# Output head of a cached-attention decode step: one product after a VectorE reduction, or four products after a ScalarE copy, with the loads of x on GpSimd's queue

## The chip, the cores and the metric

One core of a Trainium2 chip runs one launch of the kernel. The core has TensorE (PE, products into PSUM), VectorE (DVE), ScalarE (ACT), GpSimd (POOL) and SyncE (SP), each with its own instruction queue, and 16 DMA engines that all queues share. The metric is device time in microseconds for one execution. Three runs of the kernel before gave 661.82, 661.88 and 662.24 us, median 661.88.

## The reference

For each of two sequences (B = 2, one new token each, D = 512) the token x goes through a layer norm. The attention branch computes q = x·wq for 32 heads of 128, and attends over a cache of 32,768 keys and values for 8 key-value heads; four query heads share one of them:

```python
scores = einsum("bhqd,bhkd->bhqk", q, k) * (Dh ** -0.5)
o = einsum("bhqk,bhkd->bhqd", softmax(scores), v)
s = o.reshape(B, Sq, Hq * Dh) @ wo
g = silu(layer norm, w3, gelu, w4, residual, of the normed x)   # the w1/w2 part is zero for one position
return x + s * g
```

With a sequence length of one, the shifted parts in front of w2 are all zero, so w1 and w2 are not read. Nearly all the data is the cache: 2 × 8 pairs of one K block and one V block, 8 MB each, in bf16.

## The kernel before, in words

The work has three stages.

**Prologue.** SP queues wq, w3, w4 and the first K block. ACT's queue loads x twice: once as two rows (`x_bf`) for the layer norm, and once as four pieces into rows 0, 32, 64 and 96 of `x4_bf` (lines 264 and 265), a layout that only the very last addition (`out4`) uses; these four wait until GpSimd has cleared `x4_bf`. The prologue computes q for all heads, lays it out as masks, and runs the small MLP branch to the gate g.

**Sixteen groups.** A group is one pair (sequence, key-value head). Its K block and V block are spread over 128 partitions, 256 keys on each. K is held in three half-block slots (`kbuf`), V in two half blocks (`vbuf`). In a group:

- DVE transposes the two halves of K in 8 steps each (L481) into four buffers `T`. It waits for K (`t_k`), and from the fifth step on for a buffer that TensorE has freed (`t_used`).
- TensorE makes the scores of each half, 32 products into a bank `sc` (L550). Late in the first half it signals `s_half`, on which SP queues the next K block.
- DVE takes row maxima (`peak`, L464 and L466), TensorE spreads them (L562), DVE forms the shift, ACT takes the exponentials (L411), DVE transposes them to `pt` (L502).
- TensorE sums the exponentials with a product with ones (L566, into `S`), and then makes the value products, 64 of them, into the bank `o` (L575). The last signals `s_pv`, on which SP queues the next V block.
- DVE reduces `S` to the denominators and takes the reciprocals `rec` (L506, L510), right after its transposes of `pt`.

**The head output.** In bank `o` each row holds four 128-wide pieces, of which one counts. What is left of group m is done inside group m + 1. SP hands on `s_pv` as `t_o`. After the fourth transposition of the first half, DVE runs `head_ob`: it waits for `t_o`, multiplies `o` by a 0/1 mask `row_t` (L442) and adds the four pieces to `obm` (L446). Between the halves TensorE makes one fp32 product (`head_oT`, L526), which adds up the rows of each head. After the fourth transposition of the second half, DVE takes the row maxima of the first half and runs `head_on`, which multiplies by `rec` (L438). TensorE spreads the result (`head_xp`, L531), and DVE and GpSimd put it into `oX`.

After the last group the same steps run once more in `pe_output`, with the output products (L599) around them: `wo` comes in three parts, rows 0 to 3, 4 to 6 and 7 of eight, each with a semaphore of its own. Sixteen products belong to each row. The products of the first part stand between `head_oT` and `head_xp`. Then DVE multiplies by the gate and adds x (L517, L518), and two small transfers write the output.

**What sets the order.** Every engine's order is written out by hand. TensorE's program is in blocks with branches: `pe_turn` sends the first turn to the prologue and the others to `pe_groups`; both end in a jump to `pe_next`, which counts the turn and goes back to `pe_turn` or on to `pe_output`. `pe_output` holds a branch with a hint behind the first part of `wo`. SP's queue is in order: for each group the K transfer waits for `s_half`, the V transfer for `s_pv`, then `t_o` is raised. The last K block and the last V block are queued as two halves each.

Of the kernel before, what the change touches and what calls it, by code (L numbers as in the profile page):

```python
# [18 lines left out]
VT = 4  # L19
# [75 lines left out]
def kernel(  # L95
# [58 lines left out]
    obm = sb("obm", [128, Dh], F32)  # L154
# [19 lines left out]
    row_t = sb("row_t", [128, VT], F32)  # L174
# [55 lines left out]
    t_d, t_o = sem("t_d"), sem("t_o")  # L230
# [15 lines left out]
    with tc.tile_critical(no_gpsimd_drain=True):  # L246
# [16 lines left out]
        e_g0 = po.op(lambda e: e.memset(g4[:, :], 0.0))  # L263
        for n in range(NQ):
            ac.op(lambda e, n=n: e.dma_start(out=x4_bf[32 * n:32 * n + B, :], in_=A_x[:, 0, n * QW:(n + 1) * QW]), e_x4z, inc=(d_x4, 16))


        ve.op(lambda e: e.memset(o[:, :], 0.0), inc=(t_o, 1))
# [29 lines left out]
        ve.op(lambda v: v.tensor_reduce(out=row_t[:, :], in_=sel_o[:, :, :], axis=AX.X, op=ALU.add), (ve.sem, ve.n))  # L298
# [89 lines left out]
        for m in range(1, NG):  # L388
# [13 lines left out]
            nc.sync.sem_inc(t_o, 1)  # L402
        for i, (a, c) in enumerate(wo_parts):
            sp.op(lambda e, a=a, c=c: e.dma_start(out=wo3[:, a:c, :], in_=wos[:, a:c, :]), (s_pv, NG - 1), inc=(d_wo[i], 16))
        sp.wait((s_pv, NG))
        nc.sync.sem_inc(t_o, 1)


        for m in range(NG):
            for i in range(NPART):  # L410
                ac.op(lambda v, i=i: v.activation(  # L411
                    out=ep[i][:, :], in_=sc[i][:, :], func=ACT.Exp, scale=inv_sqrt_dh, bias=shift[:, :], accum_out=rs[:, i:i + 1]),
                    (s_shift, m + 1), e_tf if m == 0 else None, inc=(t_e, 1))

# [21 lines left out]
        def head_on():  # L436
            take(nc.vector, t_oT, 2)
            nc.vector.tensor_mul(out=on[:, :], in0=oT[:, :], in1=rec[:, :]).then_inc(t_on, 1)  # L438

        def head_ob():  # L440
            take(nc.vector, t_o)
            nc.vector.tensor_mul(  # L442
                out=ob[:, :].rearrange("p (t d) -> p t d", t=VT), in0=o[:, :].rearrange("p (t d) -> p t d", t=VT),
                in1=row_t[:, :].unsqueeze(2).broadcast_to([128, VT, Dh])).then_inc(t_d, 1)
# [25 lines left out]
        ve.op(lambda v: v.memset(rec[:, :], 1.0), inc=(t_oT, 1))  # L470
        with nc.Fori(0, NG // 2, engines=[DVE], hint_back_edge=True):
            for par in range(2):
                for i, h in enumerate(order(par)):
# [3 lines left out]
                    for r in range(NR):  # L477
# [6 lines left out]
                        if i == 0 and r == 3:  # L484
                            head_ob()
# [10 lines left out]
                for i, h in enumerate(order(par)):  # L496
# [8 lines left out]
                take(nc.vector, t_S)  # L505
                nc.vector.tensor_reduce(  # L506
                    out=den[:, :], in_=S[:, 0:NPART * rep].rearrange("p (i h) -> p h i", h=rep),
# [139 lines left out]
```

## Time and profile before

| | |
|---|---|
| median of three runs | 661.88 us |
| the profiled execution | 662.16 us, span of the trace 660.0 us |
| TensorE products busy | 423.8 us, 64% of the span |
| VectorE busy | 404.0 us, 61% |
| ScalarE busy | 29.6 us, 4% |
| GpSimd busy | 9.7 us, 1% |
| data read | 280.50 MB, 425 GB/s over the span |
| granted TensorE clock, mean | 0.828 |

The span is the time from the first to the last instruction of the trace; 2.16 us of the execution lie outside it. All times below are microseconds from the start of the span. In a row of the timeline the columns are start, duration, engine, line, operation, output and inputs, how many instructions are merged, and in brackets the idle time before the row with what ended it. "DVEq" or "PEq" there means that the engine's own queue was waiting on a semaphore.

### The profile page before, as it was taken

How to read it: one execution, taken by the hardware profiler on the slowest of the kernel's cores; microseconds unless marked ns; L12 is line 12 of the kernel's file. 1: busy time of each engine (PE TensorE's matmuls, PEld its weight loads, DVE VectorE, ACT ScalarE, POOL GpSimd, SP SyncE). 2: the span in 40 equal slices, each digit the busy share in tenths (PEclk: the TensorE clock that was granted, in tenths of full speed). 3: DMA queues.
4: the chain of work that ended last, by engine and by line, in shares of the span. 5: the costliest groups of instructions: out<-in, count | busy, mean ns of one | idle time of the engine just before them, and what ended most of it. 6: DMA issues, size and time to landing. Idle time of an engine off the chain costs nothing. (4 is left out here: it accounts for less than half of the span.)

```text
span 660.0 us, 6591 instructions
## 1 busy us (share of the span) xinstructions
PE 423.8 (64%) x2412; PEld 151.6 (23%) x2412; DVE 404.0 (61%) x571; ACT 29.6 (4%) x72; POOL 9.7 (1%) x42
## 2 busy tenths in 40 slices
PE   1637396666739666684965668496566848656965
PEld 0112132222213222221321222132122213212323
DVE  5349293773929477392946739294673919468761
ACT  1100000000000000000000000000000000000000
POOL 1000000000000000000000000000000000000000
PEclk9859788796978879697877969677796977779897
DMA  8999999999999999999999999999999999999994
GB/s 361 442 438 441 445 437 421 417 445 441 445 433 417 425 445 441 441 429 422 429 445 441 441 421 429 429 445 441 437 425 429 429 445 441 433 425 419 435 414 167
DMA packets 6458, 280.57 MB, mean 425 GB/s; under 512 B 682, under 2 KB 692, under 8 KB 1716
## 3 DMA queue, kind: packets, MB, share of 16 engines
q1 hardware_dynamic: 6408, 280.50, 98.3%
q8 instruction: 2, 0.03, 0.0%
q14 instruction: 4, 0.03, 0.0%
q10 hardware_dynamic: 44, 0.01, 0.0%
HBM read 280.50 MB, written 0.00 MB: 425 GB/s over the span
## 5 line engine op out<-in xcount | busy, mean ns | idle before, releaser
L481 DVE STREAM_TRANSPOSE T<-kbuf 128x1024 int32<-128x1024 int32 x256 | 293.9, 1210 | 151.7 <-DVEq L461 151.7
L550 PE MATMUL sc<-T,z 128*128 128x512 bf16 x1024 | 295.8, 424 | 137.1 <-PEq L461 128.2
L550 PEld LDWEIGHTS sc<-T,z 128*128 128x128 bf16 x1024 | 92.6, 103 | 325.8 <-issue 268.0
L575 PE MATMUL o<-vbuf,pt 128*16 128x512 bf16 x1024 | 92.7, 542 | 0.0
L411 ACT ACTIVATE ep<-sc,shift 128x512 bf16<-128x512 f32 x32 | 21.7, 683 | 581.0 <-DVE shift L495 581.0
L575 PEld LDWEIGHTS o<-vbuf,pt 128*16 128x16 bf16 x1024 | 30.8, 119 | 54.2 <-issue 47.2
L566 PE MATMUL S<-sm,ones_f 128*128 128x8 f32 x32 | 9.0, 354 | 51.8 <-PEq L461 51.8
L502 DVE STREAM_TRANSPOSE pt<-ep 128x512 bf16<-128x512 bf16 x32 | 22.6, 708 | 15.3 <-DVEq L461 15.3
L464 DVE TENSOR_REDUCE mx<-sc 128x1 f32<-128x512 f32 x32 | 21.5, 672 | 15.7 <-DVEq L461 15.7
L562 PE MATMUL S<-mxr,same_h 128*128 128x64 f32 x32 | 6.5, 284 | 22.0 <-PEq L461 22.0
L566 PEld LDWEIGHTS S<-sm,ones_f 128*128 128x128 f32 x32 | 7.9, 307 | 53.5 <-issue 53.5
L446 DVE TENSOR_REDUCE obm<-ob 128x128 f32<-128x512 f32 x17 | 17.7, 1040 | 2.5
L442 DVE TENSOR_TENSOR ob<-o,row_t 128x512 f32<-128x512 f32 x17 | 11.2, 656 | 7.6 <-DVEq L461 7.6
L562 PEld LDWEIGHTS S<-mxr,same_h 128*128 128x128 f32 x32 | 4.8, 188 | 29.8 <-issue 29.8
L506 DVE TENSOR_REDUCE den<-S 128x4 f32<-128x8 f32 x16 | 2.7, 167 | 13.7 <-DVEq L461 13.7
L466 DVE TENSOR_SCALAR mxr<-row_of,mx 128x32 f32<-128x32 f32 x32 | 7.7, 241 | 4.8
L431 POOL COPY oX<-oXs 128x4 bf16<-128x4 bf16 x15 | 2.9, 191 | 517.6 <-DVE oXs L458 517.6
L493 DVE TENSOR_REDUCE top<-S 128x1 f32<-128x64 f32 x16 | 3.6, 224 | 11.2 <-DVEq L461 11.2
L526 PEld LDWEIGHTS oT<-sel_h,obm 128*128 128x128 f32 x34 | 6.3, 188 | 5.4 <-issue 2.7
L329 PE MATMUL sc<-kbuf,xT 128*2 128x512 bf16 x32 | 3.6, 627 | 5.5 <-DMA kbuf<-in_A_wq_dram 5.5
L366 PE MATMUL sc<-vbuf,h_bf 128*2 128x512 bf16 x14 | 4.9, 522 | 2.4 <-DVE h_bf L363 2.4
L420 POOL TENSOR_TENSOR z<-qr,quad 128x64 bf16<-128x64 bf16 x16 | 4.7, 294 | 107.6 <-DVE shift L495 90.4
(80 smaller groups left out, 73.8 us busy)
## 6 DMA issues: line engine op xcount, KB each, us to landing
kbuf<-in_A_k_cache_dram SPq DMA_DIRECT2D x2, 4096.0 KB, 22.0
vbuf<-in_A_v_cache_dram SPq DMA_DIRECT2D x2, 4096.0 KB, 18.6
kbuf<-in_A_wq_dram SPq DMA_DIRECT2D x1, 4096.0 KB, 13.5
vbuf<-in_B_w_dram SPq DMA_DIRECT2D x2, 1792.0 KB, 19.2
kbuf<-in_A_wo_dram SPq DMA_DIRECT2D x1, 2048.0 KB, 27.6
kbuf<-in_A_wo_dram SPq DMA_DIRECT2D x1, 1536.0 KB, 31.0
kbuf<-in_A_wo_dram SPq DMA_DIRECT2D x1, 512.0 KB, 31.7
kbuf<-in_A_k_cache_dram SPq DMA_DIRECT2D x15, 27.0
```

The source lines that it names most:

```text
L411: ac.op(lambda v, i=i: v.activation(out=ep[i][:, :], in_=sc[i][:, :], func=ACT.Exp, scale=inv_sqrt_dh, bias=shift[:, :], accum_out=rs[:, i ...
L442: nc.vector.tensor_mul(out=ob[:, :].rearrange("p (t d) -> p t d", t=VT), in0=o[:, :].rearrange("p (t d) -> p t d", t=VT), in1=row_t[:, :]. ...
L446: nc.vector.tensor_reduce(out=obm[:, :], in_=ob[:, :].rearrange("p (t d) -> p d t", t=VT), axis=AX.X, op=ALU.add).then_inc(t_ob, 1)
L464: nc.vector.tensor_reduce(out=mx[:, i:i + 1], in_=sc[i][:, :], axis=AX.X, op=ALU.max).then_inc(t_d, 1)
L466: ins = nc.vector.tensor_scalar_mul(out=mxr[:, i, :], in0=row_of[:, :], scalar1=mx[:, i:i + 1])
L481: nc.vector.transpose(out=Ts[n % T_BUFS][:, :].rearrange("p (b t k) -> p t b k", b=NB, t=RT), in_=kt[:, r * W:(r + 1) * W].rearrange("p (t ...
L502: nc.vector.transpose(out=pt[h][:, :, :].rearrange("p r (t h) -> p t r h", h=rep), in_=ep[i][:, :].rearrange("p (t r h) -> p t r h", r=NR, ...
L526: nc.tensor.matmul(oT[:, :], lhsT=obm[:, :], rhs=sel_h[:, :], start=True, stop=True).then_inc(t_oT, 1)
L550: ins = nc.tensor.matmul(sc[i][:, :], lhsT=z[:, nb, w, zc:zc + 128], rhs=Tb[:, nb, :, w], start=(r == 0 and nb == 0 and w == 0), stop=(r = ...
L562: nc.tensor.matmul(S[:, NPART * rep:], lhsT=same_h[:, :], rhs=mxr[:, :, :].rearrange("p i r -> p (i r)"), start=True, stop=True).then_inc( ...
L566: nc.tensor.matmul(S[:, 0:NPART * rep], lhsT=ones_f[:, :], rhs=sm[:, :, :].rearrange("p i h -> p (i h)"), start=True, stop=True).then_inc( ...
L575: ins = nc.tensor.matmul(o[32 * j:32 * j + VT * rep, :], lhsT=pt[h][:, r, a * VT * rep:(a + 1) * VT * rep], rhs=vt[:, u * VT:(u + 1) * VT, ...
```

## The change

Four things are altered.

- GpSimd instead of ACT issues the four small loads of x into `x4_bf`, behind its clearing operations. One more clearing, of `ob`, goes ahead of them.
- `head_ob` with its mask `row_t` is gone. ACT copies the bank `o` to `ob` after each group, waiting for `s_pv` itself, so SP's relay `t_o` is gone too. TensorE's `head_oT` makes four fp32 products that accumulate, one for each 128-wide piece, with the selecting matrix `sel_o` in the place of `sel_h`.
- The sum of the exponentials is made after the value products instead of before them. The reduction to denominators and the reciprocal move from the end of the group into `head_on`, in the next group; `S` starts as ones.
- TensorE's program loses the block `pe_next` and the hinted branch: a group ends in the count and the branch itself, `pe_output` is one piece, and the prologue stands last in memory.

```diff
@@ prologue @@
+        po.op(lambda e: e.memset(ob[:, :], 0.0), inc=(t_ob, 1))
         for n in range(NQ):
-            ac.op(lambda e, n=n: e.dma_start(out=x4_bf[32 * n:32 * n + B, :], in_=A_x[:, 0, n * QW:(n + 1) * QW]), e_x4z, inc=(d_x4, 16))
-        ve.op(lambda e: e.memset(o[:, :], 0.0), inc=(t_o, 1))
+            po.op(lambda e, n=n: e.dma_start(out=x4_bf[32 * n:32 * n + B, :], in_=A_x[:, 0, n * QW:(n + 1) * QW]), e_x4z, inc=(d_x4, 16))
+        ve.op(lambda e: e.memset(o[:, :], 0.0))
+        ve.op(lambda e: e.memset(S[:, 0:NPART * rep], 1.0), inc=(t_S, 1))
...
-        ve.op(lambda v: v.tensor_reduce(out=row_t[:, :], in_=sel_o[:, :, :], axis=AX.X, op=ALU.add), (ve.sem, ve.n))
@@ SP @@
             load_v(m, (s_pv, m))
-            nc.sync.sem_inc(t_o, 1)
...
-        sp.wait((s_pv, NG))
-        nc.sync.sem_inc(t_o, 1)
@@ ACT, each group @@
+            ac.op(lambda v: v.copy(out=ob[:, :], in_=o[:, :]), (s_pv, m + 1), inc=(t_ob, 1))
@@ DVE @@
         def head_on():
+            take(nc.vector, t_S)
+            nc.vector.tensor_reduce(
+                out=den[:, :], in_=S[:, 0:NPART * rep].rearrange("p (i h) -> p h i", h=rep),
+                axis=AX.X, op=ALU.add).then_inc(t_d, 1)
+            take(nc.vector, t_d)
+            nc.vector.reciprocal(out=rec[:, :], in_=den[:, :]).then_inc(t_oT, 1)
             take(nc.vector, t_oT, 2)
             nc.vector.tensor_mul(out=on[:, :], in0=oT[:, :], in1=rec[:, :]).then_inc(t_on, 1)
-        def head_ob():
-            take(nc.vector, t_o)
-            nc.vector.tensor_mul(
-                out=ob[:, :].rearrange("p (t d) -> p t d", t=VT), in0=o[:, :].rearrange("p (t d) -> p t d", t=VT),
-                in1=row_t[:, :].unsqueeze(2).broadcast_to([128, VT, Dh])).then_inc(t_d, 1)
-            take(nc.vector, t_d)
-            nc.vector.tensor_reduce(
-                out=obm[:, :], in_=ob[:, :].rearrange("p (t d) -> p d t", t=VT), axis=AX.X, op=ALU.add).then_inc(t_ob, 1)
...
@@ TensorE @@
         def head_oT():
             take(nc.tensor, t_ob)
-            nc.tensor.matmul(oT[:, :], lhsT=obm[:, :], rhs=sel_h[:, :], start=True, stop=True).then_inc(t_oT, 1)
+            for t in range(VT):
+                ins = nc.tensor.matmul(
+                    oT[:, :], lhsT=ob[:, t * Dh:(t + 1) * Dh], rhs=sel_o[:, t, :],
+                    start=(t == 0), stop=(t == VT - 1))
+            ins.then_inc(t_oT, 1)
...
             take(nc.tensor, t_pt, NPART)
-            nc.tensor.matmul(
-                S[:, 0:NPART * rep], lhsT=ones_f[:, :], rhs=sm[:, :, :].rearrange("p i h -> p (i h)"),
-                start=True, stop=True).then_inc(t_S, 1)
...
             ins.then_inc(s_pv, 1)
-            nc.br("pe_next", engines=[PE])
+            nc.tensor.matmul(
+                S[:, 0:NPART * rep], lhsT=ones_f[:, :], rhs=sm[:, :, :].rearrange("p i h -> p (i h)"),
+                start=True, stop=True).then_inc(t_S, 1)
+            nc.regs_alu(turn, turn, 1, op=ALU.add)
+            nc.br_lt(turn, NG + 1, on_true="pe_turn", on_false="pe_output", engines=[PE])
...
-            in_next_block = nc.tensor.mark_branch_hint_location()
             head_oT()
             for i, (a, c) in enumerate(wo_parts):
                 if i == 1:
-                    nc.tensor.br_ne(turn, 0, "pe_output_2", "pe_turn").branch_hint(in_next_block)
-                    nc.switch_bb("pe_output_2")
                     head_xp()
```

More of the change, by code (lines that the diff above doesn't have):

```diff
@@ L153 @@
     den = sb("den", [128, rep], F32)
-    obm = sb("obm", [128, Dh], F32)
     mx = sb("mx", [128, NPART], F32)
@@ L504 @@
                         in_=ep[i][:, :].rearrange("p (t r h) -> p t r h", r=NR, h=rep)).then_inc(t_pt, 1)
-                take(nc.vector, t_S)
-                nc.vector.tensor_reduce(
-                    out=den[:, :], in_=S[:, 0:NPART * rep].rearrange("p (i h) -> p h i", h=rep),
-                    axis=AX.X, op=ALU.add).then_inc(t_d, 1)
-                take(nc.vector, t_d)
-                nc.vector.reciprocal(out=rec[:, :], in_=den[:, :]).then_inc(t_oT, 1)
-        head_ob()
         head_on()
```

10 lines of the change are left out of this document (2 added, 8 removed).

## The prediction, made before the result was known

> **What bounds the kernel now.** I read the stream of data first: the page's DMA queues and issues, the table of stretches, and the waits of SP's queue.
>
> ```profile
> q1 hardware_dynamic: 6408, 280.50, 98.3%
> kbuf<-in_A_k_cache_dram SPq DMA_DIRECT2D x15, 27.0
> vbuf<-in_A_v_cache_dram SPq DMA_DIRECT2D x15, 24.3
> 100.00:200.00 100.00, 61.57 (x361) 22.03 (x362) 56.70 (x80) 4.34 (x12) 1.46 (x6) 0.83 1.00 433
> SPq L380 <- PE o L575: 303.2, 14, 22.4
> ```
>
> SP's queue keeps the 16 DMA engines busy for 98.3% of the span. In the middle they move 433 GB/s, so a block of 8.39 MB takes 19.4 us. A K block lands 27.0 us after its issue and a V block 24.3: they are queued 7.6 and 4.9 us before the engines reach them. SP waits for TensorE (`s_pv`, 303.2 us in 14 waits) and still issues in time. In the middle of the run, then, no engine's work can shorten the time, and none lengthens it unless it delays an issue by more than 4.9 us. What is left is the start and the end. The end is read from the landings of the last blocks, the timeline from group 14 (the last but one) on, and the chain of waits.
>
> ```profile
> L397 SPq DMA_DIRECT2D kbuf<-in_A_k_cache_dram x2: 328/374/420, 594.8 to 595.2; - x2
> ...
> DMA to landing us min/median/max: 17.4/22.0/26.7
> L385 SPq DMA_DIRECT2D vbuf<-in_A_v_cache_dram x2: 327/380/433, 617.6 to 618.0; - x2
> ...
> DMA to landing us min/median/max: 13.9/18.6/23.2
> L404 SPq DMA_DIRECT2D kbuf<-in_A_wo_dram x3: 388/507/4286, 618.5 to 619.5; - x3
> ...
> DMA to landing us min/median/max: 27.6/31.0/31.7
> ...
> 650.89 1.66 PE pro L599 x64
> 652.55 0.20 PE xp L531 x4
> 652.75 1.59 PE pro L599 x54
> 654.34 1.14 issue
> 655.47 0.35 PE pro L599 x10
> ```
>
> The rows of L397 (last K), L385 (last V) and L404 (`wo`) give the first and last issue, and from issue to landing least, median and most. First issue plus least and last issue plus most: the halves of K land at 612.2 and 621.9, those of V at 631.5 and 641.2, the first and third part of `wo` at 646.1 and 651.2, and the second, a median of 31.0 behind an issue near 618.9, at 649.9. The other rows are the chain that ended last, in order of time (start, duration, what). The last data is there at 651.2, but the output products end at 655.82: at the end the kernel is 4.6 us behind its data, held by a chain of engines. That chain is what the change can touch.
>
> **The change part by part.** First the chain through the last two groups.
>
> ```profile
> 587.85 0.65 DVE L442 TENSOR_TENSOR ob<-o,row_t 128x512 f32<-128x512 f32 x1
> 589.60 9.12 DVE L481 STREAM_TRANSPOSE T<-kbuf 128x1024 int32<-128x1024 int32 x8
> 611.09 6.47 PE L575 MATMUL o<-vbuf,pt 128*16 128x512 bf16 x64
> 612.26 4.62 DVE L481 STREAM_TRANSPOSE T<-kbuf 128x1024 int32<-128x1024 int32 x4 [0.46 <-DVEq L461]
> 617.49 3.79 PE L550 MATMUL sc<-T,z 128*128 128x512 bf16 x16
> 618.61 0.69 DVE L442 TENSOR_TENSOR ob<-o,row_t 128x512 f32<-128x512 f32 x1 [1.72 <-DVEq L461]
> 620.42 9.12 DVE L481 STREAM_TRANSPOSE T<-kbuf 128x1024 int32<-128x1024 int32 x8
> 641.38 0.50 PEld L566 LDWEIGHTS S<-sm,ones_f 128*128 128x128 f32 x2 [3.35 <-issue]
> 641.90 6.42 PE L575 MATMUL o<-vbuf,pt 128*16 128x512 bf16 x64
> 642.12 0.17 DVE L506 TENSOR_REDUCE den<-S 128x4 f32<-128x8 f32 x1 [0.86 <-DVEq L461]
> 642.43 0.18 DVE L510 RECIPROCAL rec<-den 128x4 f32<-128x4 f32 x1
> ```
>
> *`head_ob` leaves DVE.* In group 14 it stands from 587.85 to 589.60: 1.75 us. *Denominators move into `head_on`*: reduction to reciprocal takes 0.31 (642.12 to 642.43), and I take the same from the reciprocal to the product, +0.62 between two rounds of transposes (bounds: the bare 0.17 + 0.18 = 0.35, and 1.2 with each of two semaphore trips as long as the 0.46 before 612.26). At the old place nobody was behind them but the next K. *The sum product moves behind the value products*, which start 0.52 earlier (641.38 to 641.90). So group 14's value products start at 611.09 − 1.75 + 0.62 − 0.52 = 609.44 and end at 615.9; the sum product takes 0.52, and the scores of group 15 start at 616.45 instead of 617.49.
>
> In group 15 `head_ob` costs more than its 1.75: DVE has made four transposes by 616.88 and then waits 1.72 us for the value products, so the fifth comes at 620.42. Without it the fifth waits for the first free buffer only, that is for 4 of the 16 products at 617.49 (3.79 × 4/16 = 0.95): 616.45 + 0.95 + 0.2 for the signal = 617.6. That is 2.8 us earlier. The next delay would be the second half of K at 621.9; DVE needs it at 617.6 + 4 × 1.14 = 622.2, just behind. With +0.62 in `head_on` and −0.52 for the sum product, the last value products start 2.7 us earlier, at 639.2. Their second half needs V at 639.2 + 3.2 = 642.4, after its landing at 641.2. They end at 648.32 − 2.7 = 645.6.
>
> *Four products instead of one* in mid-group: the page's row of L526 (below) counts two weight loads of 188 ns for each of the 17 products, so three more are 1.1 us on TensorE between the halves. DVE paces there, its four buffers (4.6 us) ahead, and `head_on` asks for the result only after four more transposes; I cost it at nothing, and at 1.1 us if that cover fails. *ACT's copy* adds a wait for `s_pv` on ACT; behind it stand the next group's exponentials, which come some 22 us later (616 to 638), so only the last copy counts. *`head_on`'s wait for the sum* holds up DVE's last four transposes, but the sum is made before the next group's first scores. *SP's relay* goes without cost, and SP's later issues were not held by it.
>
> Then the tail.
>
> ```profile
> 638.88 0.69 ACT L411 ACTIVATE ep<-sc,shift 128x512 bf16<-128x512 f32 x1 [29.37 <-DVE shift L495]
> L526 PEld LDWEIGHTS oT<-sel_h,obm 128*128 128x128 f32 x34 | 6.3, 188 | 5.4 <-issue 2.7
> 650.50 0.30 PEld L526 LDWEIGHTS oT<-sel_h,obm 128*128 128x128 f32 x2 [2.68 <-issue]
> 650.53 0.36 PE L526 MATMUL oT<-sel_h,obm 128*128 128x4 f32 x2 [2.21 <-PEq L461]
> ```
>
> Before, the relay, mask and sum take 2.18 us, from the last value product (641.90 + 6.42 = 648.32) to 650.50. After, an ACT pass over the same 128x512 bank: 0.69 by L411's row, 0.1 to 0.2 to start it, 0.1 to hand on: 0.95, to 646.55 (bounds: 0.69 alone, and 2.18 if it is as slow as the old path). The sum product, 0.52, runs beside it on TensorE. Four products at 0.32 each (one, from its first weight load to its end at 650.89, is 0.39, and the load of the next overlaps) end at 647.85 (bounds: 0.28 and 0.45 each, −0.2 and +0.5). Part one of `wo` has landed; 64 products, 1.66: 649.5. `head_xp` 0.20: 649.7. Part two lands at 649.9: a new wait of 0.2. Its 48 products at 1.59/54 = 0.029 us: 651.35. Part three has landed at 651.2; 16 products: 651.85.
>
> *The pause of 1.14 us* at 654.34 is no wait for data: 54 products had run since 652.75, 48 of part two and six of part three, and no semaphore stands between the sixteen of part three. The count of DMA queues has a row for instructions; here it stands for the whole span, for the window 0 to 5 and for the window 653 to 655.
>
> ```profile
> q8 instruction: 2, 0.03, 0.0%
> ...
> q8 instruction: 1, 0.02, 1.3%
> ...
> q8 instruction: 1, 0.02, 3.0%
> ```
>
> One such transfer comes at the start, when TensorE enters the prologue, one in the pause, none in the sixteen groups between. I read it as code of the output fetched when it was reached. After the change the output stands ahead of the prologue, so that the code behind the groups is needed, and fetched, at the start. I cost the pause at zero; the bounds are zero and 2.5 us (653, where the window begins, to 655.47, if nothing ran beside the fetch). [...]
>
> Sum against 655.82: value products −2.7, copy for relay, mask and sum −1.2, three more products +0.9, wait for part two +0.2, pause −1.1, together −3.9; by the times themselves 651.85 − 655.82 = −3.97, **−4.0 us**. Behind it L517, L518 and the write stay as they are. The profiled execution, 662.16, becomes 658.2; it lies 0.28 above the median, so against 661.88 I forecast **658.0 us**. It can't come much lower: part three at 651.2 and 16 products end at 651.65.
>
> **The start.**
>
> ```profile
> 1.53 1.19 ACTq L265 DMA_DIRECT2D x_bf<-in_A_x_dram  x4
> 20.21 0.29 POOL L420 TENSOR_TENSOR z<-qr,quad 128x64 bf16<-128x64 bf16 x1 [17.23 <-DVE qr L343]
> 32.22 0.21 DVE L374 CAST x<-x_bf 128x128 f32<-128x128 bf16 x1
> 42.41 4.62 DVE L481 STREAM_TRANSPOSE T<-kbuf 128x1024 int32<-128x1024 int32 x4 [9.33 <-DVEq L461]
> 32.38 2.50 ACTq L373 DMA_DIRECT2D g<-g  x4
> q10 hardware_dynamic: 4, 0.00, 0.0%
> ```
>
> ACT's four issues took 1.19 us and delayed only a table load. On GpSimd they come after its clearing operations, from about 3 us on; behind them in its queue is `z`, at 20.21, which TensorE reads only after 42.41. No row shows what an issue on GpSimd costs: from 0.3 us each, as on ACT, to some 10 us each before `z` would be late. The cast of x at 32.22 did not wait, and DVE's next work that counts comes at 42.41, when K lands: 10 us of cover. I take nothing. The clearing of `S`, the mask `row_t` and the first `rec` on DVE lie in the same stretch.
>
> **Rivals.** *The output's code is fetched late on the new path too.* For it: the pause exists. Against it: the transfer at the start and none in the groups. Price 1.14 to 2.5: 659.1 to 660.5. *The chain gains less and TensorE's and ACT's added steps eat it*: `head_on` at 1.2, copy at 2.18, products at 0.45 and the pause kept: 658.0 + 0.6 + 1.2 + 0.5 + 1.1 = 661.4, which is no difference (a measurement of this kernel tells about 0.2%, 1.3 us, from none). It needs all bounds at once. *Slower: x lands late.* Small loads queue behind the stream: of the four loads of g issued from 32.38 to 34.88, packets still moved after 50 (the last row, window 50 to 60), some 18 us. Four loads issued by about 8 would so be in at 26. Every microsecond after 42.4 starts the groups later; 7.6 are covered by the second K block's place in the queue and 4.0 by the gain, so beyond 54 the kernel is slower; at 57 it is 665. [...]
>
> **How the numbers follow.** Forecast 0.65 (657.2 to 659.2); code fetch 0.14; no difference 0.07; x late 0.09; slower stream 0.05. Faster 0.79, same 0.07, slower 0.14. The two slower cases, 0.14, and the tails are left out; the rest reaches from 657.2, below the bound by the last landing by half a microsecond, to 661.4.
>
> **What would show it.** No DVE row between the fourth and fifth transposes; the fifth of group 15 near 617.6; last value products near 639.2; L599 without a pause, its last products right behind the landing at 651.2. Wrong if the landings themselves move, if x's cast at 32.22 comes later than 42, or if a packet of the instruction queue stands in the tail.

## The result and the profile after

The changed kernel takes 659.29 us, median of six executions (658.06 to 660.09), against 661.85 for six of the kernel before beside it: a ratio of 0.9958, 95% interval 0.9946 to 0.9971. It is faster, by 0.42%, and the forecast of 658.0 is 1.3 us too low: the median lies 0.09 us above the 657.2 to 659.2 of the forecast's main case, and inside the 657.2 to 661.4 that the forecast spans. A second set of six, taken later, gave 658.18 (658.04 to 659.85) and a ratio of 0.9947 (0.9926 to 0.9968). The executions spread over two microseconds; what lies behind this spread is the subject of most of the experiments. The profiled execution is the slowest of the first six: 660.09, with a span of 658.3 where the prediction's sum gave 656.0 (660.0 − 4.0).

The end first: the timeline of the changed kernel, last group and output (start, duration, engine, line, what; in brackets the idle time before it and what ended it).

```profile
614.23 9.13 DVE L474 STREAM_TRANSPOSE T<-kbuf 128x1024 int32<-128x1024 int32 x8 [2.97 <-DVEq L455]
...
624.05 4.62 DVE L474 STREAM_TRANSPOSE T<-kbuf 128x1024 int32<-128x1024 int32 x4 [0.70 <-DVEq L455]
...
629.55 0.16 DVE L435 TENSOR_REDUCE den<-S 128x4 f32<-128x8 f32 x1
...
630.33 4.62 DVE L474 STREAM_TRANSPOSE T<-kbuf 128x1024 int32<-128x1024 int32 x4
...
641.34 5.37 PE L560 MATMUL o<-vbuf,pt 128*16 128x512 bf16 x64 [3.39 <-PEq L455]
...
646.76 0.59 ACT L410 COPY ob<-o 128x512 f32<-128x512 f32 x1 [6.65 <-PE o L560]
...
647.49 1.03 PE L511 MATMUL oT<-sel_o,ob 128*128 128x4 f32 x8 [0.46 <-PEq L455]
...
648.45 1.06 PE L585 MATMUL pro<-kbuf,oX 128*2 128x128 bf16 x64
...
649.44 0.25 PE L519 MATMUL xp<-on,sel_r 128*128 128x4 bf16 x4
...
652.05 1.87 PE L585 MATMUL pro<-kbuf,oX 128*2 128x128 bf16 x64 [2.36 <-DMA kbuf<-in_A_wo_dram]
```

DVE makes its first eight transposes of the last K block in one stretch, where before four were followed by 1.72 us of waiting and by `head_ob`. Behind them it waits 0.70 us for the second half of K, which by the trace landed at 623.8. The copy stands right behind the value products, four fp32 products behind the copy (the row counts two passes for each), and the second half of the output products runs without a pause. The last row's bracket is the new thing: TensorE has idled for 2.36 us, and what ended that is data. Before, the last products ran 4.6 us behind the last landing. The row of the `wo` loads (the changed kernel's line L402) gives first and last issue, and from issue to landing least, median and most.

```profile
L402 SPq DMA_DIRECT2D kbuf<-in_A_wo_dram x3: 433/507/7352, 617.4 to 618.4; - x3
...
DMA to landing us min/median/max: 30.8/34.1/34.7
```

The last part of `wo` lands at 618.4 + 34.7 = 653.1 and the products end at 652.05 + 1.87 = 653.92, 0.8 behind it. What TensorE waited for is the second part (chain of waits):

```profile
617.83 34.09 DMA kbuf<-in_A_wo_dram
651.92 0.14 issue
```

From its landing at 651.92 to the end of the 64 products are 2.0 us; the forecast had 649.9 and 651.85. The chain at the end is as short as forecast. But before, that landing was at 651.2: the data itself is 1.9 us later. The data is late from the first K block on, which shows in the first transposes, as DVE idles until the block lands (timeline at the start):

```profile
44.29 13.70 DVE L474 STREAM_TRANSPOSE T<-kbuf 128x1024 int32<-128x1024 int32 x12 [12.87 <-DVEq L455]
```

Before it was 42.41. The 1.9 us arise ahead of 44 and are never made up: q1, the queue of the loads, fills 98.7% of the 16 engines' span, and the lateness is still 1.9 at the end. What is new ahead of 44 is in the table of DMA queues: the rows of the instruction queue q8 and of the software queue for the whole span, and that of q8 in the window 28 to 33 (packets, MB, share of the time of 16 engines in the window).

```profile
q8 instruction: 7, 0.11, 0.1%
...
q0 software_dynamic: 128, 0.00, 0.0%
...
q8 instruction: 2, 0.03, 4.4%
```

Before, this queue had two transfers in the whole run (near 4 and 653), here it has seven, at 2.1, 9.0, 30.9, 31.2, 74.5, 653.0 and 658.0 by the trace, 16,384 B each. That they are TensorE's code is a reading: the trace does not say whose code a transfer carries, but the runs below change them by changing TensorE's blocks alone. Two come together 2.3 us after TensorE has ended its prologue (28.6) and goes back to the loop, and 4.4% of 16 engines for 5 us are 3.5 us for the two, 1.4 and 2.1. In the runs below, a transfer near 31 that met no other took 0.93 to 0.96; the one near 2, amid the first loads, took 1.5 to 1.9 without meeting another (1.9% to 2.4% in the window 0 to 5, six profiles). The 128 packets of the software queue are the loads of x by GpSimd, whose row has its four issues and the times from issue to landing:

```profile
L264 POOL DMA_DIRECT2D x_bf<-in_A_x_dram x4: 521/524/704, 3.4 to 5.1; - x4
...
DMA to landing us min/median/max: 7.6/9.2/10.4
```

So there are two suspects for the late landings: the code transfers near 31 (theory A), and GpSimd's queue (theory B).

The landings narrow the place down. The trace has 16 landing signals for each load, which I read as one for each DMA engine; a block counts as landed with the last of them. For the load of weights that ends at 23 us, the latest two signals are 1.31 and 1.45 us behind the median one; in the first run below, with x on ScalarE, it is 1.02 and 1.35. At the first K block they are 2.70 and 3.25 behind here, 1.19 and 1.31 there, while the median signal comes at 40.9 and 40.8. By that reading two engines of sixteen lose their time, and they lose it between 23 and 41 us.

### The profile page after: what moved, and what is told of

Read it like the earlier page. It is cut to its first block, busy times and chain, and to the rows that moved or that the text cites. A ratio compares the mean times of both kernels' runs of the same rounds, so it can differ in the third digit from the quotient of the medians.

```text
span 658.3 us, 6698 instructions
## 1 busy us (share of the span) xinstructions
PE 411.1 (62%) x2498; PEld 167.2 (25%) x2514; DVE 376.8 (57%) x538; ACT 38.9 (6%) x88; POOL 12.4 (2%) x47
## 3 DMA queue, kind: packets, MB, share of 16 engines
q1 hardware_dynamic: 6408, 280.50, 98.7%
## 5 line engine op out<-in xcount | busy, mean ns | idle before, releaser
L538 PE MATMUL sc<-T,z 128*128 128x512 bf16 x1008 | 280.7, 428 | 141.5 <-PEq L455 137.2
L538 PEld LDWEIGHTS sc<-T,z 128*128 128x128 bf16 x1024 | 101.0, 105 | 301.6 <-issue 220.6
L560 PE MATMUL o<-vbuf,pt 128*16 128x512 bf16 x1024 | 90.5, 531 | 54.2 <-PEq L455 54.2
L560 PEld LDWEIGHTS o<-vbuf,pt 128*16 128x16 bf16 x1024 | 32.9, 117 | 106.0 <-issue 98.6
L511 PEld LDWEIGHTS oT<-sel_o,ob 128*128 128x128 f32 x136 | 17.7, 191 | 3.2 <-issue 0.5
L511 PE MATMUL oT<-sel_o,ob 128*128 128x4 f32 x136 | 16.2, 243 | 0.5 <-PEq L455 0.5
L410 ACT COPY ob<-o 128x512 f32<-128x512 f32 x16 | 9.4, 586 | 111.1 <-PE o L560 111.1
L519 PE MATMUL xp<-on,sel_r 128*128 128x4 bf16 x68 | 4.1, 164 | 4.4 <-PEq L455 4.3
L567 PEld LDWEIGHTS S<-sm,ones_f 128*128 128x128 f32 x32 | 4.8, 188 | 6.9 <-issue 6.9
L407 ACT ACTIVATION_READ_ACCUMULATOR ep<-sc,shift 128x1 f32 x32 | 6.3, 196 | 0.0
## 6 DMA issues: line engine op xcount, KB each, us to landing
kbuf<-in_A_wo_dram SPq DMA_DIRECT2D x1, 512.0 KB, 34.7
```

Of the source, the lines that this page charges most:

```text
L407: ac.op(lambda v, i=i: v.activation(out=ep[i][:, :], in_=sc[i][:, :], func=ACT.Exp, scale=inv_sqrt_dh, bias=shift[:, :], accum_out=rs[:, i ...
L410: ac.op(lambda v: v.copy(out=ob[:, :], in_=o[:, :]), (s_pv, m + 1), inc=(t_ob, 1))
L511: ins = nc.tensor.matmul(oT[:, :], lhsT=ob[:, t * Dh:(t + 1) * Dh], rhs=sel_o[:, t, :], start=(t == 0), stop=(t == VT - 1))
L538: ins = nc.tensor.matmul(sc[i][:, :], lhsT=z[:, nb, w, zc:zc + 128], rhs=Tb[:, nb, :, w], start=(r == 0 and nb == 0 and w == 0), stop=(r = ...
L560: ins = nc.tensor.matmul(o[32 * j:32 * j + VT * rep, :], lhsT=pt[h][:, r, a * VT * rep:(a + 1) * VT * rep], rhs=vt[:, u * VT:(u + 1) * VT, ...
L567: nc.tensor.matmul(S[:, 0:NPART * rep], lhsT=ones_f[:, :], rhs=sm[:, :, :].rearrange("p i h -> p (i h)"), start=True, stop=True).then_inc( ...
```

## The experiments

"Together" below means that the two code transfers near 31 us overlap in the profile.

**Who issues x.** First the changed kernel with ScalarE instead of GpSimd as the issuer, and then the kernel before with GpSimd as the issuer.

```diff
-            po.op(lambda e, n=n: e.dma_start(out=x4_bf[...], in_=A_x[...]), e_x4z, inc=(d_x4, 16))
+            ac.op(lambda e, n=n: e.dma_start(out=x4_bf[...], in_=A_x[...]), e_x4z, inc=(d_x4, 16))
```

> The changed kernel with the four loads of x back on ACT's queue, nothing else. In the trace of the changed kernel the last two of the 16 engines land the first K block 2.7 and 3.3 us behind the median engine (0.9 and 1.5 before), and the lateness stays, so the last part of wo lands at 653.1 instead of 651.2. Theory A (code): two code transfers near 31 us, when TensorE goes back from the prologue, held up two engines. Then nothing moves here: lateness of the first K block about 3 us, two code transfers near 31, time 659.3 +- 0.8. Theory B (queue): GpSimd's loads made two engines late. Then the lateness falls to 1.5, the last part of wo lands near 651.2, and the time is 658.0.

658.44 us (658.01 to 659.51), ratio 0.9954 (0.9939 to 0.9969), beside 661.61 before. In the profiled execution (658.17, span 656.4) one code transfer stands in the window 28 to 33, and nothing is late: the transposes start at 42.23. The window's row, and from the chain of waits the last landing and the products behind it:

```profile
q8 instruction: 1, 0.02, 1.2%
```

```profile
617.25 33.99 DMA kbuf<-in_A_wo_dram
651.25 0.14 issue
651.38 0.62 PE pro L585 x15
```

Without lateness the last value products start at 639.48, where the prediction had 639.2, and the output products end at 652.0; the prediction had 651.85. Two of the other five executions took over 659, as some of the changed kernel do.

> The kernel before with GpSimd issuing the four loads of x, nothing else. Theory A (code): no code transfer near 31, lateness of the first K block 1.5 us, time 661.9 +- 0.4. Theory B (queue): lateness about 3, last landing near 653, time 662.5 to 663.5.

The kernel before with the opposite edit: 661.53 (659.06 to 663.8), ratio 0.9997 (0.9985 to 1.0009). No difference, no code transfer near 31, transposes from 42.39. In its profile the pause ahead of the last ten products is there as before, 1.36 us. The loads of GpSimd alone delay nothing that can be measured.

**The order of TensorE's blocks.** The kernel before, without the block `pe_next` and without the hinted branch, and nothing else changed. In the source text the prologue stands behind the output in both kernels; that it stands last in memory only without `pe_next` is the premise of this section, and no trace shows it. "New order" below means without `pe_next`, "old order" with it.

```diff
             ins.then_inc(s_pv, 1)
-            nc.br("pe_next", engines=[PE])
+            nc.regs_alu(turn, turn, 1, op=ALU.add)
+            nc.br_lt(turn, NG + 1, on_true="pe_turn", on_false="pe_output", engines=[PE])
...
-                    nc.tensor.br_ne(turn, 0, "pe_output_2", "pe_turn").branch_hint(in_next_block)
-                    nc.switch_bb("pe_output_2")
...
-            nc.br("pe_next", engines=[PE])
-        with nc.body("pe_next", valid_engines=[PE]):
...
-            nc.br_lt(turn, NG + 1, on_true="pe_turn", on_false="pe_output", engines=[PE])
+            nc.br("pe_turn", engines=[PE])
```

> The kernel before with TensorE's blocks in the order of the changed one (prologue last, no block for the count, no hinted branch), the head unchanged. Theory A (code): code transfers near 31 us and about 3 us of lateness; the pause of 1.1 us among the last output products is gone; the chain before it is that of before, so the products end near 654.7 and the time is 660.8 (659.9 to 661.9). Theory B (queue): no lateness beyond 1.5, and the same gain from the pause, 660.7. Rival to my reading of the pause: it is not code, stays, and the time is 661.9 or more.

661.36 (658.77 to 664.92), ratio 1.0002 (0.9984 to 1.0021). The chain at the end has no pause any more:

```profile
650.96 0.20 PE xp L531 x4
651.15 1.37 PE pro L597 x61
652.52 0.03 issue
```

The new order takes the pause away. That the pause was code fits all five profiles that have one, here and below: in each the products go on 1.26 to 1.39 us behind the end of the code transfer in the tail (before: 653.14 + 0.96 = 654.10, products from 655.47).

Yet the median shows no gain (the interval leaves room for 1 us), and the twelve executions lie further apart (6.2 us) than those of before beside them (659.86 to 662.63). The profiled one is among the quickest: its output products end at 652.52, 3.3 us ahead of before, and the pause is only 1.1 of that. The value products of the last two groups take 5.21 and 5.79 us; before they took 6.47 and 6.42, and in the last run of all, which has the same TensorE program and only x issued by GpSimd, 6.41 and 6.39. The granted clock differs with them. The rows are those of group 14 in this run and in that last one, each with its line in the table of stretches (there the third number from the end is the granted clock):

```profile
611.04 5.21 PE L575 MATMUL o<-vbuf,pt 128*16 128x512 bf16 x64
611.04:616.25 5.21, 5.21 (x66) 1.85 (x66) 4.38 (x6) 0.00 (x0) 0.00 (x0) 0.69 1.02 440
...
611.60 6.41 PE L575 MATMUL o<-vbuf,pt 128*16 128x512 bf16 x64
611.60:618.01 6.41, 6.41 (x66) 2.16 (x66) 4.97 (x6) 0.00 (x0) 0.00 (x0) 0.56 0.99 429
```

Duration times clock is 3.6 in both. With the head of before the end hangs on these products, so the time depends on the clock that an execution is granted there. With the new head they end ahead of the data: in its nine profiles the value products of the last group take 5.3 to 6.1 us, and TensorE still waits 0.8 to 2.5 us for the second part of `wo`. That this is why executions of the old head spread over several microseconds is likely, not shown, since those that weren't profiled have no rows.

Here too code transfers come near 31: two between 28 and 33, this time apart (28.4 and 30.7), 2.3% in the window's row instead of 4.4%, 0.93 us each, and the transposes start in time, at 42.42.

```profile
q8 instruction: 2, 0.03, 2.3%
```

**A head that is smaller, with the old order.** The changed kernel with `ob`, `sel_o`, `sm`, `ones_f`, `mxr` and `same_h` in bf16, and with `pe_next` back (without the hinted branch); x is issued by ScalarE. Each product of the head is then a single weight load: the groups by line have 68 loads of 96 ns for the 68 products, where the changed kernel has 136 of 191 ns.

```diff
-    ob = sb("ob", [128, VT * Dh], F32)
+    ob = sb("ob", [128, VT * Dh], BF16)
...
-            nc.regs_alu(turn, turn, 1, op=ALU.add)
-            nc.br_lt(turn, NG + 1, on_true="pe_turn", on_false="pe_output", engines=[PE])
+            nc.br("pe_next", engines=[PE])
```

> [...] Theory A (code): no transfer near 31, lateness 1.5 at the first K block and about 0.9 at the end, last part of wo at 651.2, output products at its heels; 657.7 to 658.3, or up to 1.1 more if the code of the last output products is again fetched when reached. It should be 1 us or more below the changed kernel with x on ACT. Theory B (queue): both the same, 658.0.

658.28 (658.20 to 658.77), ratio 0.9949 (0.9936 to 0.9963). Six executions within 0.6 us; no code transfer near 31, transposes from 42.22. The pause is back, but what is left of it is 0.51 us (chain of waits). Reckoned back from the products at 651.90, with the 1.26 to 1.39 behind a transfer and some 0.96 for the transfer, I estimate that the transfer began near 649.6, ahead of the last landing at 650.98.

```profile
617.08 33.90 DMA kbuf<-in_A_wo_dram
650.98 0.14 issue
651.12 0.27 PE pro L585 x5
651.39 0.51 issue
651.90 0.51 PE pro L585 x11
```

The same with x issued by GpSimd:

> The kernel with the head in bf16 in the block order of before, the four loads of x on GpSimd instead of ACT; that kernel on ACT had 658.28 (658.20 to 658.77), narrow enough to see half a microsecond. Theory A2: loads of x cost nothing, no code transfer near 31: 658.3 +- 0.3. Theory C: 658.8 to 659.2.

658.41 (658.13 to 658.53, seven executions), ratio 0.9951 (0.9932 to 0.997), no code transfer near 31, transposes from 42.46. GpSimd's issue costs nothing that can be measured with the new head either.

**The changed kernel again**, beside these:

> The changed kernel once more, beside the others on one chip. The first trace had two code transfers near 31 us, 0.26 apart, that took 1.4 and 2.1 us, and the last part of wo at 653.1; with x on ACT one of 0.9 us, and wo at 651.2. Theory A2 (code, by chance): how late an engine becomes depends on whether the code transfers meet on one engine that is behind already, so it differs from execution to execution; times between 658.0 and 660.1, and lateness of the first K block and time of the last landing go together. Theory C (GpSimd's loads cost 0.8 us in every execution): 659.3 again, and the kernel with x on ACT is at 658.4.

658.18 (658.04 to 659.85). The profiled execution is the one of 659.85. The window 28 to 33 and the first transposes:

```profile
q8 instruction: 2, 0.03, 4.6%
```

```profile
44.14 13.63 DVE L474 STREAM_TRANSPOSE T<-kbuf 128x1024 int32<-128x1024 int32 x12 [11.14 <-DVEq L455]
```

Together again, and late again; the five executions that weren't profiled took 658.04 to 658.70, beside the forecast of 658.0.

**The place of the sum product.** The changed kernel with the sum product ahead of the value products, and the denominators at their old place:

```diff
+            nc.tensor.matmul(
+                S[:, 0:NPART * rep], lhsT=ones_f[:, :], rhs=sm[:, :, :].rearrange("p i h -> p (i h)"),
+                start=True, stop=True).then_inc(t_S, 1)
...(value products)
-            nc.tensor.matmul(
-                S[:, 0:NPART * rep], lhsT=ones_f[:, :], rhs=sm[:, :, :].rearrange("p i h -> p (i h)"),
-                start=True, stop=True).then_inc(t_S, 1)
```

> The changed kernel with the sum product again ahead of the value products and the denominators right behind it, at the end of the group. By the prediction's terms the last value products start 0.52 later for the last group and 0.52 for the one before, and head_on is 0.62 shorter twice; so the start of the last value products moves by -0.2 to +0.5. The output waits for wo part two in the changed kernel, so the time should move by no more than +0.3: 658.3 to 659.6. If the value products were still what the end hangs on, +0.5.

658.75 (657.99 to 660.11), ratio 0.9961 (0.9946 to 0.9975): nothing that can be told from the changed kernel. The profiled execution (659.99) has the transfers together (4.4%) and its transposes from 44.22. Then the reverse, the kernel before with only the sum product moved behind the value products and the denominators in `head_on`:

> The kernel before with only the sum product moved behind the value products and the denominators into head_on; mask and sum stay on DVE, block order as before. By the prediction's terms the value products of group 14 and 15 start 0.52 earlier each and head_on grows by 0.62; the wait of DVE for the value products of group 14 goes with them: last value products 0.0 to 0.4 earlier, the sum product beside DVE's mask and sum costs nothing, pause as before: 661.2 to 661.8. So this part alone brings almost nothing, and the gain of the change must lie with mask and sum leaving DVE.

664.32 (663.36 to 667.09), ratio 1.0044 (1.0027 to 1.0061): slower, where I expected no difference. The rows of the last group (timeline):

```profile
613.79 4.62 DVE L487 STREAM_TRANSPOSE T<-kbuf 128x1024 int32<-128x1024 int32 x4 [1.18 <-DVEq L468]
...
642.59 0.70 DVE L508 STREAM_TRANSPOSE pt<-ep 128x512 bf16<-128x512 bf16 x1
...
643.59 1.88 PE L572 MATMUL o<-vbuf,pt 128*16 128x512 bf16 x16 [3.39 <-PEq L468]
```

The value products start 0.30 us after the last transposition of the weights (643.59 − 643.29). For the kernel before the same two rows give 640.56 + 0.70 and 641.90: 0.64. The move gains 0.34, not 0.52, as the wait for the signal stays, and `head_on` takes back 0.63. From the first transposition of the last K block to the last value products it is 29.80 here and 29.64 before. The rest of the loss is not in that chain: the last K block lands 1.5 us later (613.79 against 612.26, DVE idle ahead of both), though no code transfer stands near 31 and the transposes start at 42.34, and the pause is 1.64 instead of 1.14. By the landings of the K blocks the loss builds up on the way: 0.16 us at 197, 1.51 at 507. Why the stream loses it I can't say.

**What brings the transfers together?** The small-head version, x on ScalarE, with nothing but the order of the blocks as in the changed kernel:

```diff
-            nc.br("pe_next", engines=[PE])
+            nc.regs_alu(turn, turn, 1, op=ALU.add)
+            nc.br_lt(turn, NG + 1, on_true="pe_turn", on_false="pe_output", engines=[PE])
...
-            nc.br("pe_next", engines=[PE])
-        with nc.body("pe_next", valid_engines=[PE]):
...
-            nc.br_lt(turn, NG + 1, on_true="pe_turn", on_false="pe_output", engines=[PE])
+            nc.br("pe_turn", engines=[PE])
```

> [...] Theory A (two code transfers near 31 us, when TensorE goes back from the prologue to the loop, and at times both at once, which leaves the last transfer engines 1.8 us late for the rest of the run): code transfers near 31 us in the profile; the times spread from 658.0 to 660.1 as those of the changed kernel do, where the version with the old order lay within 658.2 to 658.8; no pause ahead of the last output products. If the profiled execution has the two transfers together, its first K block's lag is near 3 us and its last landing near 653.2; if it has one or two apart, 1.3 and 651.2. Rival (the order of the blocks has no effect on the start): no transfer near 31 us or no effect of it, 658.0 to 658.6 in every execution.

658.50 (657.83 to 658.86), ratio 0.9952 (0.9939 to 0.9966). The transfers near 31 are there, at 28.4 and 30.7, so the order brings them, here the loss of `pe_next` alone. They came apart, the window's row has the 2.3% of two undisturbed transfers, and the execution of 657.83 is one of the shortest of all. None of the five reached 659, so the spread that I expected did not show.

The old order with the few instructions that count the groups pushed further back, behind one branch more and a block that is never entered:

```diff
-            nc.br("pe_next", engines=[PE])
+            nc.br("pe_gate", engines=[PE])
...
+        with nc.body("pe_gate", valid_engines=[PE]):
+            nc.br_lt(turn, 99, on_true="pe_next", on_false="pe_pad", engines=[PE])
+        with nc.body("pe_pad", valid_engines=[PE]):
```

> [...]

658.15 (657.71 to 658.95), ratio 0.9947 (0.9932 to 0.9962). The queue's row for the whole span:

```profile
q8 instruction: 2, 0.03, 0.0%
```

Two transfers in all, at 4.0 and 31.0, and none in the fifteen later turns. Of the two outcomes that I had set down, transfers in many turns with 660 to 690 us, and one transfer more near the first turn with 658.0 to 658.8, the second came. The second transfer came alone at 31.0, took 0.96, and delayed little (transposes from 42.66; 42.22 and 42.46 in the two runs of the old order with the small head). There is no pause in the tail either, and no transfer in it (window 640 to 660).

All three profiles with the transfers together had GpSimd as the issuer of x, all others with the new order ScalarE. The last two runs test that: the version with the small head and the new order, and the kernel before with the new order, each with GpSimd as the issuer.

> The small-head version with the changed kernel's order of TensorE's blocks, and the four loads of x issued by GpSimd instead of ScalarE: of the version of the run before it, only the issuer of x differs. In the profiles so far the two code transfers after TensorE's prologue came together at 30.8 to 31.2 us in all three that had GpSimd issue x (the changed kernel twice, and with the sum first), with landings 1.8 us late; where ScalarE issued x they were apart (28.4 and 30.7) or only one was seen, without lateness. Theory A (the time at which the request meets the data decides, and that is a matter of one execution): together or apart, times from 658.0 to 660.1, or 657.8 to 658.9 as with ScalarE. Theory B (GpSimd's issue of x, with this order of blocks, brings the two together): together, first K block's lag near 3 us, last landing near 653, the profiled time 659.5 to 660.1, and a median above 658.7.

658.39 us (ratio 0.9957, 0.9944 to 0.997): 658.14, 658.20, 658.37, 658.41, and 659.97, 660.24. The profiled one, 658.14, has a single transfer near 31, and its transposes start at 42.55.

```profile
q8 instruction: 1, 0.02, 1.2%
```

> The kernel before with its prologue last in TensorE's memory (as in the run with the block order alone), and the four loads of x issued by GpSimd. Theory A: as the block order alone, 661.4, within 0.6, transfers together or apart. Theory B: the two code transfers together near 31 us, landings 1.8 us late, a median of 662.5 to 663.5.

661.58 (660.02 to 664.59), ratio 1.0005 (0.9992 to 1.0018), again one transfer near 31, transposes from 42.41, no pause; as the order alone. Theory B as put falls: GpSimd as the issuer does not suffice to bring the transfers together. That it makes them meet more often is not excluded: with the new head and the new order 11 of 28 executions took over 659.0 with GpSimd as the issuer, 2 of 11 with ScalarE. What the profiles of all kernels show side by side (share: the instruction queue's in the window 28 to 33):

| kernel | order | x by | transfers near 31, share | transposes from | profiled, us |
|---|---|---|---|---|---|
| before | old | ScalarE | none | 42.41 | 662.16 |
| before, x moved | old | GpSimd | none | 42.39 | 661.59 |
| before, sum last | old | ScalarE | none | 42.34 | 664.06 |
| before, order | new | ScalarE | 2 apart, 2.3% | 42.42 | 659.09 |
| before, order and x | new | GpSimd | 1, 1.2% | 42.41 | 661.23 |
| changed | new | GpSimd | 2 together, 4.4% | 44.29 | 660.09 |
| changed, again | new | GpSimd | 2 together, 4.6% | 44.14 | 659.85 |
| changed, sum first | new | GpSimd | 2 together, 4.4% | 44.22 | 659.99 |
| changed, x moved | new | ScalarE | 1, 1.2% | 42.23 | 658.17 |
| small head | old | ScalarE | none | 42.22 | 658.25 |
| small head, x | old | GpSimd | none | 42.46 | 658.27 |
| small head, count moved | old | ScalarE | 1, 1.2% | 42.66 | 658.20 |
| small head, order | new | ScalarE | 2 apart, 2.3% | 42.51 | 657.83 |
| small head, order and x | new | GpSimd | 1, 1.2% | 42.55 | 658.14 |

The late start goes with the overlap: all three profiles with it have one, none of the eleven others has; neither the order nor the issuer alone brings it. In the three, the latest two landing signals of the first K block are 2.7 to 3.3 us behind the median one, in the eleven at most 1.8. With the new head, the profiled executions with the overlap took 659.85 to 660.09, those without 657.83 to 658.27. The times of the executions that weren't profiled fit, though nothing shows what their transfers did: of those with the new head and the new order (changed kernel twice, x moved, sum first, small head with the order, and with x), 10 of 33 took over 659.0 (with the profiled ones 13 of 39); of those with the new head and the old order, none of 14 (17).

## Why the prediction was right, and where it was off

The sign held, and so did the mechanism at the end of the kernel. That the first median came out at 659.29 and not near 658.2, as the second, is partly luck: four of the first six executions took over 659, one of the second six. It is also near the price of the rival "the output's code is fetched late" (659.1 to 660.5), but no pause of that kind came. The sum itself gives 661.88 − 3.97 = 657.9; 658.0 is a rounding up. Step by step, measured in the profile of the changed kernel:

- *`head_ob` leaves DVE, and its wait in the last group goes.* From the first transposition of the last K block to the last value products: 612.26 to 641.90 before, 29.64 us; 614.23 to 641.34 after, 27.11. The gain is 2.5, the term was 2.7; in the run with x on ScalarE, whose data is in time, the last value products start at 639.48 instead of 641.90, 2.4. The fifth transposition starts some 4.6 us after the first instead of 8.2; but part of this only makes DVE idle longer ahead of the block, as it is out of work when the data comes, and the second half of K, which the prediction had just in time, is now waited for (0.70). The 0.2 for a signal in that step was my estimate, and no row shows it.
- *Denominators in `head_on`*: 629.55 to 630.33 holds three operations, 0.78, where the one at 630.41 took 0.15 before the next transposes: +0.63, forecast +0.62.
- *The sum product behind the value products*: 0.34 by the run that moved it alone, forecast 0.52. Together with the denominators it brings nothing, and the run that undid both in the changed kernel differed by nothing. So, by elimination, the gain lies with mask and sum leaving DVE for the copy and the four products; no run makes that move alone.
- *The copy on ACT*: 0.59 instead of 0.69, and 0.14 from its end (647.35) to the first product behind it (647.49), where I had taken 0.1.
- *Four products*: 1.03 against 1.28. The 64 products of the first part of `wo`: 1.06 against 1.66. This second difference is the clock and not the change: the granted clock was 1.00 here (648 to 651) and 0.50 before (651 to 653). The sum took every time of TensorE as it stood in one profile, at the clock granted there. Both gains go into the wait for the second part, 2.36 instead of 0.2, and are worth nothing, as the data is the bound: the end comes 2.0 us behind the second part of `wo` in this profile (forecast 1.95), and in the one with x on ScalarE 0.76 behind the third (652.01 − 651.25; the prediction's floor had 0.45).
- *The pause goes with the order.* It does, in every version with the new order. But the transfer in the tail does not: the changed kernel has one at 653.0, and every version with the new order one between 649.9 and 653.7, with no pause beside it. That the code behind the groups is fetched at the start, on which the zero rested, was my estimate: no trace says what a transfer carries. What the runs show is a pause of 0.15 to 1.64 us in the profiles that have one, and none with the new order.
- *The start: "I take nothing", and code "fetched at the start" at zero.* Here is the step that failed. For the loads of x it was right: each issue kept GpSimd for 0.56 us (four in 2.25), the data was in by 15.5 (5.1 + 10.4), and the two runs that moved the issue alone to GpSimd found 0.9997 and, with the small head, the same median within 0.2 us. For the code it was wrong. I had not counted on transfers at 31 us, amid the stream, 2.3 us behind the prologue's last product; the trace shows the transfers, not their reason. In some executions (13 of 39, if the times over 659.0 are taken for them) the two transfers meet, the landings are 1.8 us late from there on, and since data is the bound at the end now, 1.8 us late at 44 are nearly 2 us late at 654.

The rival "the output's code is fetched late" was wrong on place: what the transfers cost is at the start, 1.9 us at the first K block. "x late" and "slower stream" fell with the two runs on the issuer; neither shows a stream that GpSimd's loads slow (0.9997 on the kernel before; 658.41 against 658.28 with the small head). I had named moved landings as what would make the prediction wrong, and that is what the first median's 1.3 us are. I had also named a packet of the instruction queue in the tail; it came, but nothing waited for it.

The change in order and the change of the head can now be priced apart. The new head with the old order gains 3.3 us (658.28 against 661.61), all that the changed kernel gains in its second set (3.35); the bf16 of that version shortens products that end ahead of the last landing in either form (the four of the head took 0.24 us with bf16 in the profile of the version with the order as well, and 1.03 in the changed kernel's). The order shows no gain: on the kernel before, two runs with it have 1.0002 (0.9984 to 1.0021) and 1.0005 (0.9992 to 1.0018), which leaves room for 1.1 and 0.5 us, no more; with the new head the pause is half hidden behind the last landing anyway, and the order seems only to add executions that end near 660. The small head with the old order and with the moved count keep below 659.0 without exception, though their medians can't be told from that of the changed kernel's second set.

What stays open: whether two code transfers meet seems a matter of when they fall among the data, but what decides it was not found; that they delay the landings is shown by the company they keep in 14 profiles, not by a run that forces them together. Three profiles show one transfer near 31 where the same TensorE program shows two in others; why is not known. Which DMA engine carries them is not in the trace. And the stream of the version with only the sum moved is 1.5 us late for a reason that I don't know.

## What to carry to other kernels

When the data is the bound at the end, a chain is worth shortening only down to the last landing; after that, look at what delays the first landing: here 1.9 us at the first K block were 1.9 us at the last part of `wo`, 610 us later. Changing the blocks of an engine's program changed its code transfers too, from two to seven here: count the transfers of the instruction queue before and after, and see at what times they fall, as a pause taken out of the tail (1.14 us here) may be paid for at the start (1.9). When a kernel's executions lie further apart than those of the kernel beside it, one profile may be one of two cases; take a second before explaining it. And the same 64 products took 5.21 us at a granted clock of 0.69 and 6.41 at 0.56: compare durations of two profiles only with the clock beside them.

## What the runs showed of the hardware that I had not expected

- Near 31 us a code transfer of 16,384 B among saturated data took 0.93 to 0.96 us alone; two that met took 1.4 to 2.1 us each, about 3.5 together. With them the latest two of the 16 landing signals of the first K block came 1.5 to 1.9 us further behind the median one than in the run with x on ScalarE, and the last part of `wo` landed 1.9 us later (653.1 against 651.2).
- With the old order the instruction queue had two transfers in the whole run, in all six profiles: with the moved count none came behind 31.0, through 15 turns and 620 us. With the new order, where the loop has no `pe_next`, it had six or seven in the six profiles whose whole span was read, one or two of them near 31 in all eight. Why is not shown.
- The same 64 value products of a group took 4.90 us (from 611.55) to 6.54 us (from 495.61) in the changed kernel's profile, as the granted clock was 0.73 and 0.55 while they ran.
- Four loads issued by GpSimd, 0.56 us each, cost nothing that can be measured: 0.9997 (0.9985 to 1.0009) on the kernel before.
